# Issuing a layer's weights two products earlier, and transposing a table part one product earlier, in a one-core FFT filter and PReLU layer

## The chip, the core and the metric

The kernel runs on one NeuronCore of a Trainium2 chip. A core has engines with a queue of their own each: TensorE (PE in the profile; its weight loads are PEld), VectorE (DVE), ScalarE (ACT), GpSimd (POOL) and SyncE (SP). Each takes its instructions in order; they wait for one another by semaphores. DMAs are issued here from GpSimd and SyncE. The metric is the device time of one execution in microseconds (us).

## The reference

Two stages, one behind the other. A global filter in the frequency domain over each of 8 sequences of 3008 positions with 256 channels, then a two-layer network with a learned slope over all 24064 rows:

```python
X = np.fft.rfft(x, axis=1)                    # x: (8, 3008, 256)
Y = X * (filt_r + 1j * filt_i)[None]          # filters: (1505, 256)
y = np.fft.irfft(Y, n=3008, axis=1).reshape(24064, 256)
h = y @ w_in                                  # (256, 2048)
g = np.maximum(h, 0) + alpha * np.minimum(h, 0)
out = g @ w_out                               # (2048, 256), float32
```

## The kernel before

The transform of length 3008 is split into 94 times 32 and done as matmuls in float16: a first set of products over 94 points (piece_a), a turn of the layout, products with the twiddle table `twf_s` (piece_b) whose result is multiplied by the filter on VectorE, the inverse products with the table `twi_s` (piece_c), another turn, and the last inverse products over 94 points (half_d and pair_d), which leave the transform's output in `yT`. The first batch goes its own way (class First): its turns are TensorE transposes instead of round trips through DRAM. Batches 1 to 7 go through `plan_fft`, which places their pieces at numbered steps of the layer's loop.

The layer works on blocks of up to 512 rows: `up` or `up4` multiply `yT` by `win_s` (L547, L570), ScalarE evicts the result to `gtb`, VectorE applies the slope, and `down` multiplies by `wout_s` (L601). The first block is done by up4 in two halves of 256 rows (L570), so that it can begin when half of batch 0's output is there; the second transforms run between the later blocks' products. The order on each engine is that of the program text (`manual_schedule`); no planner changes it.

The change lies in the opening, ahead of the first block. Its loop (L476 to L501) runs over twelve pieces `kp`. Each turn issues piece_b(kp + 2): 16 small matmuls (L355), then the filter product `uu` on VectorE (L360). It then issues piece_c(kp): 16 matmuls (L382) with the inverse table. Every second turn the results are evicted by keep_c, and turn_at (L343) transposes the next two or more parts. So piece_b(0) and (1), ahead of the loop, give the first two `uu`, and turn kp gives the one numbered kp + 3 when counted from one.

Two things are laid into that loop. `inverse_table(16, ...)` (L419 to L424) makes entries 16 to 23 of the inverse table `twi_s` by four transposing matmuls of `twf_s` (L421) and an eviction by ScalarE; `swapped(16, nc.gpsimd)` (L426 to L429) makes from them, on GpSimd, the table `twx_s` with halves swapped, which lies in `gtb`. Both are first used by piece_c(8). The other thing are the weight loads: a memset of one column of `win_s` on VectorE (L483), then on GpSimd the loads of `win_s` (two DMAs, L485), of batch 1's `xs` (L118, eight DMAs by load_x) and of `wout_s` (two DMAs, L488). The memset writes to the tile that the DMA fills, so the first load of `win_s` waits for it, and with it GpSimd's queue, in which the other loads stand behind. They convert float32 to float16 on the way.

The psum tiles: `hps` has two buffers (psH), used by piece_b's results and by the layer's products; `psF` has one, used in turn by turn_at, by inverse_table(16) and by others; `op` has two (psO), used by piece_c.

Behind the loop come the copies of the filter into `filts_s` and `filt_s` (L504, L506, on GpSimd, for batches 1 to 7), the first transposes half_t, and half_d(0) and half_d(2), which make `yT` for the first rows, both channel halves. The first up4 needs these and both halves of `win_s`.

Of the kernel before, what the change touches and what calls it, by code (L numbers as in the profile page):

```python
# [51 lines left out]
def kernel(  # L52
# [10 lines left out]
    nc = tc.nc  # L63
# [48 lines left out]
    def load_x(b, c, held=False):  # L112
        xs = p_x.tile([128, 8 * D], FP16, name="xs")
        if held:
            for r in (slice(0, 32), slice(64, 96)):
                nc.vector.memset(xs[r, 0:2], 0.0)
        for r in (slice(0, 48), slice(48, N1)):
            nc.gpsimd.dma_start(out=xs[r], in_=xrow(b, c)[r])  # L118
        return xs
# [25 lines left out]
    def banks(wide):  # L145
        if wide:
            return psH.tile([128, 2, 512], FP32, name="hps")
        return psF.tile([128, 2, 512], FP32, name="psF")
# [155 lines left out]
    def on_act(o, i):  # L304
        nc.scalar.activation(o, i, AF.Copy)  # L305
# [113 lines left out]
    def inverse_table(ka, pb):  # L419
        for i in range(4):  # L420
            nc.tensor.matmul(pb[:, 128 * i : 128 * i + 128],  # L421
                             twf_s[:, ka + 2 * i : ka + 2 * i + 2].rearrange("p k m -> p (k m)"), id16,
                             start=True, stop=True)
        on_act(twi_s[:, ka : ka + 8].rearrange("p k m -> p (k m)"), pb)  # L424

    def swapped(ka, eng):  # L426
        t, o = twi_s[:, ka : ka + 8], twx_s[:, ka : ka + 8]
        eng.tensor_scalar(o[:, :, 32:64], t[:, :, 0:32], gs_s, None, OP.mult)
        eng.tensor_scalar(o[:, :, 0:32], t[:, :, 32:64], gs_s, -1.0, OP.mult, OP.mult)  # L429
# [6 lines left out]
    def warm(n, pw):  # L436
        for _ in range(n):
            nc.tensor.matmul(pw.rearrange("p (r c) -> p r c", r=4), id16,
                             id16.unsqueeze(1).to_broadcast([128, 4, 128]), start=True, stop=True)
# [36 lines left out]
    for kp in range(12):  # L476
        if kp < 10:
            f0.piece_b(kp + 2)
        if kp == 1:
            inverse_table(16, banks(False)[:, 0])  # L480
            swapped(16, nc.gpsimd)
        if kp == 7:
            nc.vector.memset(win_s[:, :, 0:1], 0.0)  # L483
            for kt in range(2):
                nc.gpsimd.dma_start(out=win_s[:, kt], in_=moe_w_in[kt * 128 : (kt + 1) * 128])  # L485
            xc[(1, 0)] = load_x(1, 0)
            for q in range(2):
                nc.gpsimd.dma_start(  # L488
                    out=wout_s[:, 8 * q : 8 * q + 8],
                    in_=moe_w_out[1024 * q : 1024 * q + 1024].rearrange("(j p) d -> p j d", p=128))  # L490
            for c in range(1, 4):
                xc[(1, c)] = load_x(1, c)
        f0.piece_c(kp)
        if kp > 9:
            f0.keep_c(kp, (on_act, on_act) if kp == 10 else both, 1)
        elif kp % 2 == 1:
            f0.keep_c(kp - 1, (on_act, on_act))
            if kp < 7:
                f0.turn_at(kp + 5, 2, on_act)
        if 7 < kp < 10:  # L500
            warm(2, banks(False)[:, 0])  # L501
    for o in range(0, 128, 64):
# [262 lines left out]
```

## Time and profile before

| | us |
|---|---|
| median of 3 runs | 776.31 (776.0 to 778.09) |
| the profiled execution | 776.38 |
| its span | 774.6 |
| TensorE busy | 762.2 (98%) |
| VectorE busy | 633.4 (82%) |
| ScalarE busy | 583.8 (75%) |
| GpSimd busy | 148.1 (19%) |
| mean granted TensorE clock | 0.998 of full speed |

The span is what the profiler saw from the first to the last instruction; the time is taken around it. Busy time is an average over stages with different limits, so the stages are looked at one by one. The chain of work that ended last follows the last instruction back to what released it, step by step, and shows which engine or load set the end. The timeline lists an engine's instructions in order, with the idle time ahead of each in brackets and what ended it. The stretches give busy time, instruction counts, the granted clock of TensorE, the share of the 16 DMA engines and the rate of the bytes moved.

### The profile page before, as it was taken

To read this page: it belongs to the slowest core of one execution; us is meant where nothing else is said; L and a number is where in the kernel's file an instruction comes from. 1 tells how busy PE (TensorE), PEld (TensorE's weight loads), DVE (VectorE), ACT (ScalarE), POOL (GpSimd) and SP (SyncE) were. 2 spreads that over 40 slices of the span, in tenths; PEclk is the share of its full clock that TensorE was granted. 3 is DMA by queue.
4 is the path that set the end of the run, shared out by engine and by line. 5 is a ranking of instruction groups with operands and counts; after the bars stand their busy time and mean duration, and the time that the engine had idled before them with its cause. 6 is when DMAs were issued, how large, how long until landed. Compare 5 with 4: busy or idle time off the path is not lost.

```text
span 774.6 us, 16602 instructions
## 1 busy us (share of the span) xinstructions
PE 762.2 (98%) x6552; PEld 511.2 (66%) x6552; DVE 633.4 (82%) x1159; ACT 583.8 (75%) x672; POOL 148.1 (19%) x278
## 2 busy tenths in 40 slices
PE   8799999999999999999999999999999999999998
PEld 4576656666666666666666666766666666766666
DVE  3788895788888998899978999899877888666663
ACT  4577787888778777787777877787876777677664
POOL 7610551131202212111201212021110112000000
PEclk9999999999999999999999999999999999999999
DMA  9696797664854449724794438743474233510111
GB/s 159 107 228 175 129 211 177 198 140 139 184 158 110 115 118 185 184 68 118 173 211 107 105 98 174 196 104 99 122 157 111 60 81 96 150 37 28 41 41 55
DMA packets 96814, 99.77 MB, mean 129 GB/s; under 512 B 12020, under 2 KB 83076, under 8 KB 96544
## 3 DMA queue, kind: packets, MB, share of 16 engines
q1 hardware_dynamic: 82048, 69.22, 32.6%
q0 software_dynamic: 14688, 29.49, 21.2%
q8 instruction: 51, 0.84, 0.4%
q14 instruction: 27, 0.22, 0.1%
HBM read 54.74 MB, written 46.66 MB: 131 GB/s over the span
## 4 chain that ended last, share of the span: by engine, by line
PE 93%; DMA 2%; ACT 2%; issue 1%; DVE 1%; POOL 1%; DVEq 0%; ACTq 0%; POOLq 0%
PE op L601 42%; PE hps L547 41%; PE psF L283 3%; PE hps L261 2%; PE psF L230 1%; PE hps L176 1%; DMA xs<-in_x_dram 1%; DMA win_s<-in_moe_w_in_dram 1%; PE hps L202 1%; DVE uu L360 1%; ACT asb L305 1%; PE hps L570 1%; ACT gtb L578 1%; POOL xs L118 0%; PE psF L399 0%
## 5 line engine op out<-in xcount | busy, mean ns | idle before, releaser
L556 ACT ACTIVATE gtb<-hps 128x1024 f16<-128x1024 f32 (+1 forms) x376 | 377.4, 1006 | 134.7 <-PE hps L547 130.9
L601 PE MATMUL op<-wout_s,gtb 128*128 128x256 f16 x3008 | 431.3, 273 | 0.0
L547 PE MATMUL hps<-yT,win_s 128*128 128x512 f16 (+1 forms) x1504 | 418.4, 375 | 0.9 <-ACT asb L305 0.3
L601 PEld LDWEIGHTS <-gtb 128*128 128x128 f16 x3008 | 290.9, 98 | 164.2 <-issue 10.7
L559 DVE TENSOR_SCALAR m<-gtb,alm_s 128x512 f16<-128x512 f16 (+1 forms) x752 | 227.2, 345 | 99.8 <-ACT gtb L556 98.2
L561 DVE TENSOR_TENSOR gtb<-gtb,m 128x2048 f16<-128x2048 f16 (+1 forms) x188 | 226.1, 1203 | 10.3
L547 PEld LDWEIGHTS <-win_s 128*128 128x128 f16 x1504 | 142.5, 98 | 55.2 <-issue 6.6
L244 POOL DMA_DIRECT2D sw<-ww x144 | 71.6, 505 | 414.6 <-DVE ww L237 408.8
L606 ACT ACTIVATE osb<-op 128x512 f32<-128x512 f32 (+1 forms) x97 | 56.6, 584 | 12.4 <-PE op L601 11.3
L305 ACT ACTIVATE asb<-hps 128x1024 f16<-128x1024 f32 (+1 forms) x56 | 56.6, 1020 | 5.7 <-PE hps L176 4.3
L305 ACT ACTIVATE v<-hps 128x1024 f16<-128x1024 f32 (+1 forms) x43 | 43.4, 1010 | 10.8 <-PE hps L261 10.6
L237 DVE TENSOR_TENSOR ww<-psF,filts_s 128x1024 f16<-128x1024 f32 x42 | 51.1, 1218 | 0.2 <-PE psF L230 0.2
L238 DVE TENSOR_TENSOR uu<-psF,filt_s 128x1024 f16<-128x1024 f32 x42 | 51.0, 1214 | 0.0
L305 ACT ACTIVATE yT<-psF 128x752 f16<-128x752 f32 x59 | 46.9, 796 | 2.0 <-PE psF L283 1.9
L283 PEld LDWEIGHTS <-zt 96*128 96x128 f16 x512 | 28.8, 98 | 5.9 <-issue 0.3
L283 PE MATMUL psF<-wi_s,zt 96*128 96x94 f16 x496 | 31.0, 205 | 0.1
L242 POOL DMA_DIRECT2D uu<-ww x24 | 19.6, 1255 | 33.3 <-DVE uu L238 25.3
L249 DVE TENSOR_TENSOR uu<-uu,sw 128x1024 f16<-128x1024 f16 x36 | 24.6, 683 | 1.0 <-DMA sw<-ww 0.4
L118 POOL DMA_DIRECT2D xs<-in_x_dram x32 | 21.7, 891 | 12.3 <-PE hps L547 4.9
L186 DVE TENSOR_TENSOR xs<-xs 47x2048 f16<-47x2048 f16 x16 | 19.5, 1219 | 0.4
L190 DVE TENSOR_TENSOR xs<-xs 47x2048 f16<-47x2048 f16 x16 | 19.4, 1209 | 0.0
L261 PE MATMUL hps<-uu,twi_s 64*64 64x256 f16 x336 | 17.3, 281 | 0.0
(88 smaller groups left out, 265.7 us busy)
## 6 DMA issues: line engine op xcount, KB each, us to landing
out_dram<-osb SPq DMA_DIRECT2D x128, 128.0 KB
v_dram<-v SPq DMA_DIRECT2D x84, 128.0 KB
zt<-v_dram SPq DMA_DIRECT2D x28, 384.0 KB
sw<-ww POOLq DMA_DIRECT2D x144, 64.0 KB, 2.8
xs<-in_x_dram POOLq DMA_DIRECT2D x44, 192.0 KB, 6.2
at<-a_dram SPq DMA_DIRECT2D x40, 192.0 KB
a_dram<-asb SPq DMA_DIRECT2D x32, 192.0 KB
a_dram<-asb SPq DMA_DIRECT2D x12, 384.0 KB
```

The lines of the kernel that those rows point to most:

```text
L237: nc.vector.tensor_mul(ww, px, fs)
L238: nc.vector.tensor_mul(uu, px, f)
L244: nc.gpsimd.dma_start(out=sw[o : o + 32], in_=ww[i : i + 32])
L261: nc.tensor.matmul(ps[64 * par : 64 * par + 64, e, 256 * h : 256 * h + 256], twi_s[r, 4 * q + 2 * h + par], u[r, par, h], start=True, stop ...
L283: nc.tensor.matmul(ps[:, m], self.zt[:, 8 * g + 4 * mh + m, dh * 128 : dh * 128 + 128], wi3_s, start=True, stop=True)
L305: nc.scalar.activation(o, i, AF.Copy)
L547: nc.tensor.matmul(self.hps[:, j % 2, 0:tn], win_s[:, kt, j * 128 : (j + 1) * 128], yT[:, kt, self.t0 : self.t0 + tn], start=(kt == 0), st ...
L556: nc.scalar.activation(g[:, 2 * i : 2 * i + 2], self.hps[:, :, 0:tn], AF.Copy)
L559: nc.vector.tensor_scalar(m[:, 2 * i + h], g[:, 2 * i + h], 0.0, a, OP.min, OP.mult)
L561: nc.vector.tensor_add(g, g, m)
L601: nc.tensor.matmul(self.op[:, si - s0], self.gts[k][:, 128 * si : 128 * si + 128], wout_s[:, k], start=(si == s0 and k == 0), stop=(si == ...
L606: nc.scalar.activation(osb[:, 0:m], self.op[:, 0:m], AF.Copy)
```

## The change

Two pieces of the opening's loop are moved; no instruction is added or taken away.

- inverse_table(16) and swapped(16) go from turn 1, between piece_b(3) and piece_c(1), to the end of turn 0, behind piece_c(0) and ahead of piece_b(3).
- The memset of `win_s` and the loads behind it go from turn 7, behind piece_b(9) (the tenth product), to turn 5, behind piece_b(7) (the eighth product).

The order on ScalarE, GpSimd and SyncE stays what it was. On TensorE the four matmuls of L421 change places with the 16 of piece_b(3). On VectorE the memset changes places with two of the products `uu`.

```diff
     for kp in range(12):
         if kp < 10:
             f0.piece_b(kp + 2)
-        if kp == 1:
-            inverse_table(16, banks(False)[:, 0])
-            swapped(16, nc.gpsimd)
-        if kp == 7:
+        if kp == 5:
             nc.vector.memset(win_s[:, :, 0:1], 0.0)
             for kt in range(2):
                 nc.gpsimd.dma_start(out=win_s[:, kt], in_=moe_w_in[kt * 128 : (kt + 1) * 128])
...
             f0.keep_c(kp - 1, (on_act, on_act))
             if kp < 7:
                 f0.turn_at(kp + 5, 2, on_act)
+        if kp == 0:
+            inverse_table(16, banks(False)[:, 0])
+            swapped(16, nc.gpsimd)
         if 7 < kp < 10:
             warm(2, banks(False)[:, 0])
```

## The prediction

> **What bounds the kernel now.** I read the page's busy times first, then the chain of work that ended last (whole, then its first 56 us), the timelines of VectorE (DVE), GpSimd (POOL) and TensorE (PE) for 25 to 52 us, and the granted clock in stretches of one window each. The page:
>
> ```profile
> span 774.6 us, 16602 instructions
> PE 762.2 (98%) x6552; PEld 511.2 (66%) x6552; DVE 633.4 (82%) x1159; ACT 583.8 (75%) x672; POOL 148.1 (19%) x278
> PE 93%; DMA 2%; ACT 2%; issue 1%; DVE 1%; POOL 1%; DVEq 0%; ACTq 0%; POOLq 0%
> ```
>
> TensorE carries 93% of the chain; from 50 us on its named waits add up to 0.9 us. There the kernel goes at TensorE's pace, and whatever starts that stage earlier moves the end by as much. What can be won lies before 52 us, where the chain leaves TensorE:
>
> ```profile
> 24.69 0.77 DVE uu L360
> 25.82 0.14 DVE uu L360
> 26.95 0.75 DVE uu L360
> 28.08 0.66 DVE uu L360
> 29.22 0.11 DVE uu L360
> 29.62 0.43 POOL win_s L485
> 30.21 7.26 DMA win_s<-in_moe_w_in_dram
> 37.51 1.46 PE hps L570 x7
> 42.60 0.87 PE hps L570 x8
> ```
>
> The reader is to see that the first layer product (L570) waits for a load, this load waited for its issue on POOL, and the issue waited for the VectorE memset of L483, which stands in VectorE's order behind ten filter products `uu` (L360). The uu starts are 1.13 us apart. The timeline says what POOL and TensorE did meanwhile:
>
> ```profile
> 29.62 1.15 POOL L485 DMA_DIRECT2D win_s<-in_moe_w_in_dram  x2 [4.33 <-DVE win_s L483]
> 34.65 0.48 ACT L305 ACTIVATE yT<-op 128x376 f16<-128x376 f32 x1 [0.35 <-PE op L283]
> 34.82 0.55 DVE L308 CAST yT<-op 128x376 f16<-128x376 f32 x1 [0.78 <-PE op L283]
> 35.19 0.27 PE L570 MATMUL hps<-yT,win_s 128*128 128x256 f16 x1 [0.41 <-ACT yT L305]
> 37.51 1.46 PE L570 MATMUL hps<-yT,win_s 128*128 128x256 f16 x7 [2.06 <-DMA win_s<-in_moe_w_in_dram]
> ```
>
> POOL stood idle 4.33 us with the load next in its queue. The other operand, yT, was complete at 34.82 + 0.55 = 35.37; TensorE ran one product of L570 (first half of win_s) and waited 2.06 us for the second half. Last the clock, by stretches of 3.4 us; columns are PE, PEld, DVE, ACT and POOL busy, granted clock, DMA share, GB/s:
>
> ```profile
> 31.00:34.40 3.40, 3.33 (x56) 2.51 (x55) 1.78 (x3) 2.28 (x6) 3.40 (x6) 1.00 0.96 165
> 34.40:37.80 3.40, 0.94 (x12) 0.60 (x11) 1.14 (x2) 0.96 (x2) 0.90 (x3) 1.00 1.06 211
> 37.80:41.20 3.40, 3.40 (x26) 2.60 (x25) 1.27 (x4) 1.40 (x2) 1.54 (x3) 0.50 1.33 192
> 41.20:44.60 3.40, 3.40 (x40) 3.12 (x38) 2.82 (x4) 2.05 (x2) 0.50 (x1) 1.00 1.41 207
> 48.00:51.40 3.40, 2.54 (x16) 1.65 (x16) 3.37 (x7) 3.19 (x5) 0.00 (x0) 1.00 1.13 254
> ```
>
> After the stretch in which TensorE was busy 0.94 of 3.40 us the clock is 0.50 for one whole stretch, then 1.00 again. A stretch busy 2.54 of 3.40 us (the last line) brought no such drop. So the wait costs twice: itself, and half speed after it.
>
> **Part 1: third table part transposed earlier.** The four matmuls of L421 for entries 16 to 23 go ahead of the 16 matmuls of piece_b(3) instead of behind. Nothing is added. Before, they start at 20.31, ScalarE (ACT) evicts at 20.75, TensorE waits for that eviction until 21.40 (turn_at needs the same psF buffer), and the fifth uu starts at 22.42, 0.24 us after the fourth ended. Now TensorE can start them once ScalarE has freed psF (eviction 18.68 + 1.02 = 19.70), in the 0.38 us in which it waits for a uu anyway: about 19.75, so eviction about 20.2 and turn_at about 20.85. Then VectorE runs its uu without that gap: the fourth starts near 20.96, the fifth at 22.1 instead of 22.42. Value taken: -0.3 us for everything VectorE feeds, yT and the memset too. Bounds: no gain if another release holds the fifth uu; a loss of 0.1 us if the table part lands only just before 20.3 (piece_b(3) would end near 21.06, the fourth uu is due at 20.96). The POOL side, `swapped(16)`, started at 23.88 behind four filter DMAs, 3 us after its input; it does not move. ACT's order does not change.
>
> **Part 2: the weight loads.** The memset passes two uu on VectorE; the twelve DMA issues behind it (two win_s, two xs of batch 1, two wout_s, six more xs) keep their order on POOL and are moved past no instruction there, and SP's queue is untouched. The memset (60 ns) now stands behind the eighth uu, and ahead of four uu, where it costs what it cost ahead of two. Its time: start of the ninth uu, 26.95 - 0.3 = 26.65, against 29.25: -2.6. POOL's queue was empty from 25.3, so the issues go at 27.0 and 27.6. The DMA engines moved 0 GB/s from 26 to 30 us, so the 7.26 us from issue to landing should hold: second half landed at 37.47 - 2.6 = 34.9. yT is complete at 35.37 - 0.3 = 35.07. So the second product goes at about 35.1 instead of 37.51: **-2.4 us**. What is late next is yT, which leaves 0.2 us of the load's lead unused.
>
> **Part 3: the clock.** TensorE then has no gap over 0.41 us between 34.4 and 37.8, and I take the drop to be gone. The chain's TensorE items within it, at full-speed rows: seven L570 1.46 to 7/8 of 0.87 = 0.76; slopes transpose 0.21 to 0.11; eight L283 0.74 to 0.41 (the row at 43.47); eight L399 0.86 to 0.68 (41.92); eight L570 1.13 to 0.87. Sum **-1.57 us**. Behind it the evictions must follow. Stepping through buffers by hand, ACT's gtb evictions (0.92 each, back to back) and VectorE's zt copies (1.22, then two of 0.64) let the fourth up4 end near 41.0 instead of 44.77, with up to 0.2 us lost to evictions; the last VectorE copy comes within 0.05 us of the product that reads it. From there to 51 us ACT and VectorE pace the work in both, all from the same earlier start.
>
> **What else shifts.** The wout_s loads (landing near 45.7, first used at 49.7) move 2.6 us earlier while their use moves 3.8: 2.8 us of cover left; if gone, TensorE waits by the excess. xs of batch 1 is used at 49.3, issued at 30.7 and, at the median 11 us, landed near 42. The filter copies (last landing near 63.5) are used by VectorE at 64.6 and by the product at 78. The narrowest is at<-a_dram for batch 1, where a weight load waited 0.2 us near 78; its saves follow ACT's evictions, so it moves along.
>
> **Sum.** -2.4 - 1.57 + 0.2 = -3.8. The profiled execution took 776.38 (span 774.6 and 1.78 around it), so 772.6; the median of the runs shown is 0.07 lower: **772.5 us**, by bounds from -2.4 (clock not regained) to -4.2 (nothing lost to evictions, a little more from part 1): 772.1 to 773.9.
>
> The Trainium skill, "TensorE: Matmul & The Clock Gate", section "What's actually happening", says that the clock is cut after an idle window of about 3.4 us, and that the window runs free of the kernel. The trace agrees in length (0.50 for 37.8 to 41.2) but not on the idle time: a stretch that was 28% busy was enough. By the page's idle window a 2.06 us gap would cut nothing, the drop would have another cause and stay, and only the 2.4 would be won, 773.9.
>
> **Rivals.**
> A. *The wait goes, the half-speed stretch stays or comes elsewhere* (the stretches' phase against the kernel is not fixed by the kernel). For it: only one drop to learn from. Against: TensorE has no other stretch so empty. -2.4 + 0 = 773.9; if also part 1 gives nothing, win_s lands at 35.2 and the gain is 2.1: 774.2.
> B. *Hidden anyway: the end of the opening is set elsewhere.* ACT idles 3.45 us before its first gtb and VectorE 3.26 us before the slopes, both behind L570, which speaks against. If DMA traffic paced the stage (over 1.0 share from 32 to 58 us), loads needed at 49 to 62 us would keep their times: the shift of 3.8 shrinks to what they allow, 0 to 1.5: 775 to 776.3.
> C. *Slower: the earlier load takes longer.* POOL writes win_s's descriptors while VectorE is in its last four uu rather than its last two, and issue to landing grows. Loads in this stage took 5.2 to 13 us. With wout_s's 12.9 us, win_s lands at 27.6 + 12.9 = 40.5, 3.0 us later than before, 779.3; it decides from 9.9 us on (the load then lands no earlier than before). For it: issues beside uu are POOL work beside VectorE. Against: filter issues beside uu took 484 to 569 ns, those of xs at the start, with VectorE all but idle, 531 on average; and the long landings were of loads queued behind others, while win_s is first.
> D. *The change does not do what it says* (memset not ahead of the ninth uu): in the changed program's order on VectorE it stands there, so no chance of its own.
>
> **How the numbers follow.** Forecast (772.1 to 773.3) 0.66; A 0.14; B 0.12 (half of it no change); C 0.08. A measurement of this kernel tells about 0.3%, 2.33 us, from no change: faster means under 773.98. Faster: 0.66 and nearly all of A, 0.79. Same: B and a rest of A, 0.13. Slower: C, 0.08. The range leaves out C and half of B; at its low end it allows 0.3 us below the lowest sum, as the three runs went 0.3 below their median: 771.6 to 775.0.
>
> **What would show it.** In the changed profile: memset near 26.6; win_s issued near 27.0 with POOL's idle before it about 2 instead of 4.33; no VectorE gap near 22.2; the second L570 product at 35.1 with at most 0.3 us wait; clock 1.00 from 34 to 45 us; the first ACT gtb near 36.1 instead of 39.07; the last L578 eviction near 45.5 instead of 49.46; everything after it shifted alike. Wrong would make it: win_s landing after 35.4, a stretch at 0.50 in spite of it, or a new TensorE wait for wout_s, xs or at between 45 and 80 us.

## The result and the profile after

The changed kernel takes 773.88 us (median of 8 runs, 773.51 to 775.89) against 776.35 for the kernel before beside it (8 runs): a ratio of 0.9967, 95% interval 0.9955 to 0.9979, so 2.5 us or 0.33% faster. The forecast was 772.5, within 771.6 to 775.0: the direction and the range held, and of the 3.8 us forecast two thirds came. The time alone would not tell why: 773.9 is also what the prediction gave for rival A, in which the wait goes whole and the half-speed stretch stays. What came of each part is read from the trace. The profiled execution's span went from 774.6 to 772.1, by the same 2.5 us.

The page of the changed kernel, its span, busy times and the chain by engine:

```profile
span 772.1 us, 16602 instructions
PE 761.2 (99%) x6552; PEld 510.5 (66%) x6552; DVE 633.4 (82%) x1159; ACT 583.9 (76%) x672; POOL 148.2 (19%) x278
PE 95%; ACT 2%; DMA 1%; issue 1%; DVE 0%; POOL 0%; DVEq 0%; ACTq 0%
```

The chain lies with TensorE for 95% instead of 93%. Its pieces in the opening (start, length, what), to set beside those shown of before:

```profile
25.55 0.10 DVE uu L360
26.67 0.11 DVE uu L360
27.07 0.43 POOL win_s L482
27.66 8.41 DMA win_s<-in_moe_w_in_dram
36.11 0.94 PE hps L570 x7
42.28 1.94 ACT gtb L578 x2
46.94 1.02 ACT gtb L578
```

The issue of `win_s` comes two filter products earlier, at 27.07 instead of 29.62. But the chain's DMA piece grew: 8.41 us from issue to landing where it was 7.26. So the seven products start 1.40 us earlier, not 2.4. The last eviction of the first block starts at 46.94 instead of 49.46, 2.52 us earlier, and that is the whole gain of the two traces: nothing behind it gave any back. The rows of before:

```profile
44.79 1.94 ACT gtb L578 x2
49.46 1.02 ACT gtb L578
```

The timelines of GpSimd, VectorE and TensorE:

```profile
27.07 1.15 POOL L482 DMA_DIRECT2D win_s<-in_moe_w_in_dram  x2 [2.07 <-DVE win_s L480]
34.72 0.55 DVE L308 CAST yT<-op 128x376 f16<-128x376 f32 x1 [0.78 <-PE op L283]
35.09 0.27 PE L570 MATMUL hps<-yT,win_s 128*128 128x256 f16 x1 [0.41 <-ACT yT L305]
36.11 0.94 PE L570 MATMUL hps<-yT,win_s 128*128 128x256 f16 x7 [0.76 <-DMA win_s<-in_moe_w_in_dram]
```

GpSimd waits 2.07 us for the memset instead of 4.33, and TensorE 0.76 us for the second half of `win_s` instead of 2.06. The load is still what ends the wait: yT was there at 35.27 (34.72 + 0.55). The granted clock, in the stretches of 3.4 us used before (behind the stretch's length come the five busy times, then the clock):

```profile
34.40:37.80 3.40, 2.24 (x25) 1.47 (x24) 1.49 (x4) 1.62 (x3) 1.08 (x3) 1.00 1.21 195
37.80:41.20 3.40, 3.40 (x42) 3.19 (x40) 3.03 (x4) 1.96 (x4) 1.01 (x2) 1.00 1.45 197
```

TensorE is busy 2.24 of 3.40 us in the first stretch (before: 0.94), and the second runs at 1.00 instead of 0.50.

### The profile page after: what moved, and what is told of

The parts are those of the page before. It is cut to its first block, busy times and chain, and to the rows that moved or that the text cites. A ratio compares the mean times of both kernels' runs of the same rounds, so it can differ in the third digit from the quotient of the medians.

```text
span 772.1 us, 16602 instructions
## 1 busy us (share of the span) xinstructions
PE 761.2 (99%) x6552; PEld 510.5 (66%) x6552; DVE 633.4 (82%) x1159; ACT 583.9 (76%) x672; POOL 148.2 (19%) x278
## 4 chain that ended last, share of the span: by engine, by line
PE 95%; ACT 2%; DMA 1%; issue 1%; DVE 0%; POOL 0%; DVEq 0%; ACTq 0%
PE op L601 42%; PE hps L547 41%; PE psF L283 3%; PE hps L261 2%; PE psF L230 1%; PE op L438 1%; PE hps L176 1%; DMA win_s<-in_moe_w_in_dram 1%; PE hps L202 1%; ACT asb L305 1%; PE hps L570 1%; ACT gtb L578 1%; PE psF L399 0%; ACT gtb L556 0%; DVE uu L360 0%
## 5 line engine op out<-in xcount | busy, mean ns | idle before, releaser
L283 PEld LDWEIGHTS <-zt 96*128 96x128 f16 x512 | 28.6, 98 | 6.0 <-issue 0.3
L283 PE MATMUL psF<-wi_s,zt 96*128 96x94 f16 x496 | 31.0, 205 | 0.1
```

Of the source, the lines that this page charges most:

```text
L283: nc.tensor.matmul(ps[:, m], self.zt[:, 8 * g + 4 * mh + m, dh * 128 : dh * 128 + 128], wi3_s, start=True, stop=True)
```

## The experiments

The theory: the wait for the second half of `win_s`, and the half-speed stretch that this wait brings, carry the gain, and part 1 gives next to nothing. What was open after the result was why the load took 1.15 us longer to land. Ratios are to the kernel before, run beside each; its own median moved between 776.35 and 778.48, so ratios from different occasions are compared with care.

### One part at a time

Part 1 alone leaves the loads in turn 7:

```diff
-        if kp == 1:
-            inverse_table(16, banks(False)[:, 0])
-            swapped(16, nc.gpsimd)
...
+        if kp == 0:
+            inverse_table(16, banks(False)[:, 0])
+            swapped(16, nc.gpsimd)
```

> Only part 1: the third table part is transposed at the end of turn 0; the loads stay in turn 7. Theory (the wait for the second half of win_s and the half-speed stretch behind it carry the gain): the memset comes 0.1 to 0.3 us earlier (28.95 to 29.15), the second product of L570 goes at 37.2 to 37.4, the granted clock still drops to 0.50 for one stretch of 3.4 us, and the time falls by 0.1 to 0.3 us, to about 776.1. Rival (the gain comes out of the transform stage, which the table part shortens): a fall of 1 us or more, to 775.3 or below.

Measured: ratio 1.0005 (0.9992 to 1.0017), no change. In its trace the gap ahead of the fifth uu is gone (eleven uu without idle time), the memset stands at 28.72 and the second product goes at 37.13 after a wait of 2.07 us: some 0.4 us ahead of before. The times do not show this, and the trace cannot lay it to the table part: in the run with the gap filled, below, the table part stands where it was, and the memset comes at 28.72 as well. The clock still drops, here for most of 37.8 to 41.2. VectorE's products, and the stretches:

```profile
17.35 12.55 DVE L360 TENSOR_TENSOR uu<-hps,filt_s 128x1024 f16<-128x1024 f32 x11 [1.14 <-DMA filt_s<-in_filt_r_dram]
```

```profile
34.40:37.80 3.40, 0.94 (x6) 0.66 (x7) 1.14 (x2) 0.82 (x2) 0.95 (x2) 0.96 1.06 212
37.80:41.20 3.40, 3.40 (x28) 2.63 (x26) 1.77 (x4) 1.40 (x2) 1.15 (x3) 0.54 1.36 189
```

Part 2 alone leaves the table part in turn 1:

```diff
-        if kp == 7:
+        if kp == 5:
             nc.vector.memset(win_s[:, :, 0:1], 0.0)
```

> Only part 2: the memset and the loads go to turn 5; the table part stays in turn 1. Theory: memset near 26.9, second half of win_s landed 1.2 to 2.3 us earlier than before (35.2 to 36.3), no stretch at 0.50, and 2.0 to 2.4 us off the time: 774.0 to 774.3, that is all but 0.1 to 0.3 of the whole change's gain. Rival (the two parts need each other): half the gain or less, 775.1 or above.

Measured: 0.9955 (0.9941 to 0.9969), not to be told from the whole change. Memset at 27.06, second half landed 8.53 us after its issue, at 36.54, clock 1.00 throughout. The loads are the change; the rival in which the parts need each other falls. TensorE was busy 1.94 of 3.40 us in its stretch from 34.4, and the clock held:

```profile
34.40:37.80 3.40, 1.94 (x22) 1.25 (x20) 1.22 (x3) 1.15 (x3) 0.73 (x2) 1.00 1.18 197
```

Where such stretches begin against the kernel differs between executions (in part 1 alone the drop began near 37.5 instead of 37.8). But wherever 3.4 us are laid in this trace from 3 us to 760, TensorE is busy for 57% of them or more (1.94 from 34.0 and from 34.8 too).

### The clock by itself

The loads stay in turn 7, and nine filling matmuls go into the time in which TensorE waits for `win_s`:

```diff
     f0.half_d(2, on_dve, "o")
+    warm(9, bank("o"))
```

> The kernel before, with nine matmuls of the identity (0.22 us each, 2.0 in all) put ahead of the first product of L570, in the time in which TensorE waits for win_s; the loads stay where they were. Theory: the second half of win_s still lands at 37.5, so the wait is not shortened, but TensorE is busy in the stretch from 34.4 to 37.8, the clock stays at 1.00, and the items behind take 1.1 us less (the difference measured between the two profiles from the first product to the last eviction of the first block): 775.2. Rival (evictions pace that stage, so the half speed cost nothing and the whole gain is the earlier load): no change, 776.3. Rival of the other side (the clock does not drop for idle time but for something else): 0.50 stays in the records and the time is unchanged.

Measured: 0.9981 (0.9968 to 0.9995), or 0.4 to 2.5 us faster, with 1.5 in the middle, though the load still took 7.32 us to land. The timeline of TensorE (the nine filling matmuls are L438; the layer's products are L571 here):

```profile
34.66 2.10 PE L438 MATMUL op<-ids 128*128 128x512 f16 x9 [0.41 <-ACT yT L305]
37.04 0.94 PE L571 MATMUL hps<-yT,win_s 128*128 128x256 f16 x7 [0.17 <-DMA win_s<-in_moe_w_in_dram]
```

and the stretches, both at full clock:

```profile
34.40:37.80 3.40, 2.97 (x17) 1.47 (x16) 1.03 (x2) 0.69 (x2) 1.03 (x2) 1.00 1.07 213
37.80:41.20 3.40, 3.40 (x39) 3.05 (x38) 2.59 (x5) 2.22 (x3) 1.07 (x3) 1.00 1.38 195
```

The paired evictions of this run:

```profile
43.21 1.94 ACT gtb L579 x2
```

From the seven products to the paired evictions it takes 43.21 - 37.04 = 6.17 us, in the kernel before 44.79 - 37.51 = 7.28, in the changed one 42.28 - 36.11 = 6.17. So the clock's part is 1.11 us, and it is idle TensorE time that brings the drop.

The mean granted clock of every execution says the same. One stretch of 3.4 us at half speed in 775 makes a mean of 0.998 (an estimate, 3.41 x 0.5 / 774.6 = 0.2%). Of the kernel before and of part 1 alone, 63 executions are on record here with their clock, and none stood above 0.998. Of the changed kernel, part 2 alone, the gap filled and the later runs but one (that with some 180 more instructions), 41 of 43 stood at 0.999 or 1.000. Of the kernel before, 24 of 51 stood at 0.996 or less, which is more than the one drop; no kept trace is of such an execution, so where they lose it stays open.

The Trainium skill, "TensorE: Matmul & The Clock Gate", section "What's actually happening", puts the cut behind an idle window of about 3.4 us; here a stretch 28% busy was enough to bring it, and a trace in which every stretch was 57% busy or more did not have it, so the measurement sets a stricter bound.

### Why the load took longer

The first guess was the traffic behind it: hold the other loads back, to turn 9 and behind a small memset of `xs`.

```diff
                 nc.gpsimd.dma_start(out=win_s[:, kt], in_=moe_w_in[kt * 128 : (kt + 1) * 128])
-            xc[(1, 0)] = load_x(1, 0)
+        if kp == 9:
+            xc[(1, 0)] = load_x(1, 0, True)
```

> The changed kernel, but only the two loads of win_s go in turn 5; batch 1's xs and wout_s are held by a small memset behind the twelfth uu (near 31.5). This asks why the second half of win_s took 8.4 us to land instead of the 7.3 of before. Theory 1 (the loads queued behind it take part of the DMA engines' rate): with nothing behind it for 4 us it lands 5 to 6.5 us after its issue at 27.7, by 34.2, ahead of yT; the second product goes at 35.3, and 0.8 us come off the changed kernel's 773.9: 773.1, unless wout_s, now landing near 45.5 to 46, or xs, near 43 to 44, becomes late for products that want them near 46 and 46: then up to 1 us is given back. Theory 2 (GpSimd writes the load's descriptors more slowly beside VectorE's products): still about 8.4 us, landing near 36, 773.9.

Measured: 0.9957 (0.9942 to 0.9972). With nothing issued behind it from 28.5 to 32.4 the second half still took 8.57 us. Theory 1 falls; the figure of theory 2 came, which the runs in turn 3 and with 112 more instructions, below, speak against:

```profile
27.97 8.57 DMA win_s<-in_moe_w_in_dram
36.55 0.05 issue
```

The trace also holds, for every DMA, when each of the sixteen DMA engines reported its share as landed, and each fetch of instructions (queue 8, 16 KB). Read from there, for the second half of `win_s` (issue and fetch in us from the span's start, the others in us after the issue):

```
                        issue   first   15th   last    fetch served at
before                  30.21    6.6     7.1    7.3    30.24
part 1 alone            29.67    6.8     7.4    7.4    29.72
gap filled              29.68    6.8     7.1    7.3    29.58
changed                 27.66    6.6     7.2    8.4    33.15
part 2 alone            28.01    6.8     7.2    8.5    33.71
win_s alone in turn 5   27.97    6.7     7.1    8.6    33.62
```

Fifteen engines took 7.1 to 7.4 us everywhere. In the three runs with the loads in turn 5 one engine came 1.2 to 1.5 us behind the rest, and there a fetch was served in the midst of the load; its packet took 0.94 to 0.97 us. In the other three the fetch was served 0.7 to 0.8 us before the first packets of `win_s` moved (30.92 in the kernel before). A fetch comes about every 256 TensorE instructions (the 50 intervals of the kernel before average 255 of those in the trace). In the changed kernel 359 lie between the third and the fourth, then 166 to the next: the fourth was served some 100 instructions, about 3 us, late. The Trainium skill, "DMA: Bandwidth & Descriptors", section "Queues, rings and completion order", says that an engine drains a whole packet of one queue before it turns to another, which would make a fetch wait behind a load and the load's rest behind the fetch; the trace shows both delays, not the turns themselves, nor which engine a fetch or a late share was on.

To move the fetches, I replaced filling matmuls at the start by short ones, which adds TensorE instructions in about the same time. The first try added some 180:

```diff
-    warm(10, bank("o"))
+    warm_short(63, bank("o"))
...
-            warm((8, 0, 6, 0)[i // 2], bank("o"))
+            warm_short((24, 0, 18, 0)[i // 2], bank("o"))
...
-    warm(5, bank("o"))
+    warm_short(15, bank("o"))
```

> The changed kernel, with 29 of its opening's idle-filling matmuls (0.22 us each) replaced by 120 short ones of about 0.07 us, so that TensorE executes some 180 more instructions ahead of turn 0 in about the same time. In the traces of the three runs with the loads in turn 5, fifteen of the sixteen DMA engines reported the second half of win_s 7.2 us after its issue and the last one 1.2 to 1.4 us later, and a fetch of 16 KB of instructions (queue 8) ran at 33.2 to 33.7 in the midst of the load; in the three with the loads in turn 7 it ran at 29.6 to 30.2, before the load's data, and all sixteen reported within 0.7 us. Theory (that fetch takes an engine from the load and delays its share): the fetches follow TensorE's progress by 256 instructions each, so they come some 2 us earlier, the one in question near 28, ahead of the load's data; then all sixteen report by 7.3 us after the issue, the second product goes at 35.3, and 0.8 us come off the changed kernel: 773.1. Rival (the lag has to do with the loads' place, beside four uu instead of two, whatever the fetch does): 8.4 us again, 773.9.

Measured: 0.9973 (0.9962 to 0.9985), landing after 8.45 us. The fetch did move ahead of the load, to 26.70, but the next came into it, at 34.25. By itself this tells nothing apart. The median, 774.82 us, is 0.9 above the changed kernel's with much the same landing; the mean clock stood at 0.998 in four of the 12 executions, which may be part of it; the rest stays open. The changed kernel's trace was taken once more:

> The changed kernel once more, for its trace. Theory (one DMA engine lags because of an instruction fetch in the midst of the load, which comes at the same place of the program each time): second half of win_s 8.2 to 8.6 us from issue to landing again, with the fetch at 33 to 34. Rival (chance): 7.2 to 7.5 in this execution. Time 773.5 to 774.6 either way.

Measured: 773.52 us; the load took 8.13 us, fifteen engines within 7.25 us, the fetch at 32.66, both a little under what was expected. The lag recurs, with 0.9 us:

```profile
27.58 8.13 DMA win_s<-in_moe_w_in_dram
```

Then with 112 instructions more, so that one fetch comes as the load begins and the next behind it:

```diff
-    warm(10, bank("o"))
+    warm_short(50, bank("o"))
...
-            warm((8, 0, 6, 0)[i // 2], bank("o"))
+            if i == 1:
+                warm_short(24, bank("o"))
+            else:
+                warm((0, 0, 6, 0)[i // 2], bank("o"))
```

> The changed kernel with 18 of its idle-filling matmuls replaced by 74 short ones: 112 more TensorE instructions ahead of turn 0 (the run with some 180 more had moved the fetch out of the load's front, to 26.7, but brought the next one into it, served at 34.25, and the load took 8.45 us again). With 112 the two fetches should be asked for near 27.9 and 32.2; asked for while the load is in flight a fetch was served some 3 us later, so the second near 35, behind the load. Theory (a fetch in the midst of the load delays one engine's share by its own length): no lag, all sixteen engines report the second half within 7.2 to 7.5 us of its issue, by 35.2, the second product of L570 waits under 0.3 us, and the time is 0.5 to 0.8 us under the changed kernel's: about 773.2. Rival (the lag belongs to a load issued while VectorE still has four products to do): 8.1 to 8.6 us again, 773.9. If the fetch still falls ahead of the load's end, nothing is told apart.

Measured: 0.9944 (0.9928 to 0.9960), 773.35 us. The kernel before took 778.48 beside it, more than on the other occasions, so the ratio makes the gain look larger; the median itself is 0.5 us under the changed kernel's, and the two spreads overlap. Fetches came at 28.04, as the load's first packets moved (28.00), and at 35.81; all sixteen engines reported between 6.7 and 7.2 us after the issue, the last at 34.44; TensorE no longer waits for `win_s` (the products are L577 here, all eight without a break):

```profile
26.69 1.15 POOL L489 DMA_DIRECT2D win_s<-in_moe_w_in_dram  x2 [2.08 <-DVE win_s L487]
34.71 1.16 PE L577 MATMUL hps<-yT,win_s 128*128 128x256 f16 x8 [0.41 <-ACT yT L305]
```

The load stands beside four uu as in the changed kernel, so its place is not the cause; the fetch in its midst is what differs, as it was in all the traces. Behind the fetch at 35.81 one engine lags 0.8 us with the loads of wout_s, which nobody waits for. Not every fetch costs a load in flight its length: in part 1 alone one at 43.62 left the second half of wout_s without a lag (its last two engines reported within 0.03 us).

### Earlier still

```diff
-        if kp == 5:
+        if kp == 3:
             nc.vector.memset(win_s[:, :, 0:1], 0.0)
```

> The changed kernel with the loads two products earlier still, in turn 3: the memset stands behind the sixth uu, near 24.5, and GpSimd, busy until 25.0, issues the two loads of win_s at 25.0 and 25.6. Theory (in the changed kernel the second half of win_s was 1.0 us behind yT): it now lands 7.3 us after its issue at 32.9, or 1.2 us later if one DMA engine lags again, in both cases ahead of yT, so the second product goes at 35.3 and 0.8 us come off the changed kernel's 773.9: 773.1. No further gain, since yT is next. Rival: the loads meet the last filter loads, which were in flight until 26.0 and are wanted by the ninth uu at 26.7; if these land later than that, VectorE waits, and yT and all behind come later by as much, up to 1.5 us: 774.6.

Measured: 772.96 us, 0.9950 (0.9933 to 0.9968). The second half landed 7.37 us after its issue, at 33.16, its memset standing ahead of six uu; a fetch was served at 32.77, near its end, and one engine came 0.4 us behind the others, which nobody waited for. VectorE did not wait for the filter loads:

```profile
25.20 1.15 POOL L482 DMA_DIRECT2D win_s<-in_moe_w_in_dram  x2
25.40 5.91 DVE L360 TENSOR_TENSOR uu<-hps,filt_s 128x1024 f16<-128x1024 f32 x5
34.84 1.16 PE L570 MATMUL hps<-yT,win_s 128*128 128x256 f16 x8 [0.41 <-ACT yT L305]
```

TensorE's wait here is for yT (ACT yT), as the step "what is late next" had it. This is the fastest median of the study. Its six times lie at or under 773.52, the changed kernel's nine at or over 773.51, but taken on another occasion, and the intervals of the two ratios overlap; so the step from turn 5 to turn 3 is shown by the trace (no wait for win_s), and by the times only as likely.

## Why the prediction was right, and where its sizes were off

- **What bounds.** Right. The memset, the issue, the load and then the first layer products set the opening; after 48 us TensorE's named waits add up to 0.9 us in the changed kernel too, and the 2.52 us won there reached the end as 2.5.
- **Part 1, -0.3 us.** The gap ahead of the fifth uu closes, as forecast. But when the filter loads land early the idle time only moves: the changed kernel's trace has 0.26 and 0.27 us ahead of the third and the fourth uu, the one with the gap filled 0.26 and 0.43 ahead of the third and the fifth. The times show no gain, and single traces cannot size one: yT was ready 0.1 us earlier in the changed kernel, 0.4 in part 1 alone, and 0.5 in the run with the gap filled, which does not have part 1.
- **Part 2, issue.** Right to a tenth: memset 26.65 forecast, 26.70 measured; issue 27.0, 27.07.
- **Part 2, landing.** This step failed. "The 7.26 us from issue to landing should hold" was argued from an idle DMA system between 26 and 30 us. It held for fifteen of sixteen engines (7.2); one came 1.2 us behind where an instruction fetch was served in the midst of the load, and the load lands with its last engine: 8.41, at 36.06. That is past the 35.4 which the prediction itself had named as a sign of being wrong. The seven products started 1.40 us earlier instead of 2.4; with the fetch moved out of the load (the run with 112 more instructions) it went as forecast: landed 7.16 us after the issue, and no wait ahead of the second product.
- **The clock, -1.57, with 0.2 lost to evictions.** The drop went, as forecast. The sum was too large: it measured 1.11. The rows taken for full speed were those of later groups, or halves of the slow ones; at this place, at a clock of 1.00, the seven L570 took 0.94 instead of 0.76, the eight L283 0.59 instead of 0.41, the slopes transpose 0.16 instead of 0.11 and the L399 0.73 instead of 0.68. The same lengths stand in the trace with the gap filled; why these groups are longer here stays open.
- **The rivals.** A did not come, though its time did: no stretch is below 1.00, and the filled gap shows that idle time was the cause. That the measured 773.88 meets A's 773.9 is chance: the late load cost 1.0 us and the clock's part came 0.3 us short (1.11 against 1.37), together about the 1.4 us by which A and the forecast differ. B did not: the loads wanted at 46 to 60 us came in time, and everything behind shifted alike. C was the right place with the wrong reason: the load did take longer, by 1.15 us, short of the 2.6 from which it decides; but not because descriptors were written beside VectorE's products, since the run in turn 3 wrote them beside such products too, and took 7.37.
- **The sum.** 1.40 + 1.11 = 2.51 us, against 2.4 + 1.37 = 3.8 forecast. The 0.2 us set aside for evictions were not needed. The forecast missed by 1.4 us of 3.8; the range held because it reached down to a gain with no clock in it at all. Two slips bear on nothing: 0.3 us under the lowest sum of 772.1 is 771.8, not 771.6, and `swapped(16)` started 2.5 us behind its input, not 3.

## What to carry to other kernels

Follow a late load back to its issue: here a 60 ns memset in a busy engine's order held a 7 us load, and moving it ahead of two products brought the whole gain. Count an idle gap of TensorE twice, itself and the half-speed stretch behind it; a gap that can't be closed can be filled. And keep a margin for an instruction fetch, up to 1.5 us here, between a load's usual landing and its first use.

## What the runs showed of the hardware

- A load lands with the last of its sixteen DMA engines, and an instruction fetch of 16 KB, served in the midst of it, put one engine 0.9 to 1.5 us behind in the two traces of the changed kernel and the three like it. Fetches came about every 256 TensorE instructions, so adding or removing TensorE instructions far ahead moves them into or out of a load: 112 more took the landing from 8.4 to 7.2 us, some 180 more left it at 8.45.
- A stretch of 3.4 us with TensorE 28% busy was followed by 0.50 of the clock for as long, in the two traces that have one. A trace in which no such stretch was under 57% busy kept 1.00. Where between them the line lies was not tried.
